# A fused attention and two-network kernel: readings of other engines' results in the first network listed half an item later

## The chip, the cores and the metric

One core of a Trainium2 chip runs the whole program. The metric is the device time of one execution in microseconds (us); the median of three runs is taken.

## The reference

Three layers run one after the other, all in float32. Shapes: batch 4, 8 heads, 768 positions, head dimension 48; so 3072 tokens of 384 numbers.

```
state = alpha[t][:, None] * state + outer(k[t], v[t]);  y[t] = q[t] @ state       # per batch and head
h = x @ w_in;  x1 = where(h > 0, h, exp(min(h, 0)) - 1) @ w_out                   # 384 -> 2048 -> 384
p = probs / (probs.sum(-1) + 1e-9)
out = sum over 4 experts e of p[:, e] * (relu(x1 @ w1[e]) @ w2[e])                # 384 -> 1024 -> 384
```

## The kernel before

**Precision.** A float32 matrix product is made of three products: each operand is kept as two parts, a rounded one ("hi") and what is left ("lo"), and hi x hi, hi x lo and lo x hi are added up in PSUM. `split` (L370) makes the parts: ScalarE (ACT) copies the source into hi (L372), VectorE (DVE) subtracts hi from the source into lo (L373).

**Tokens.** They are cut into 6 chunks of 512 (4 batches of 128 positions). A *unit* is one batch of one chunk in the attention layer. Chunk 0's four units run in a prologue. After it the first network runs as 96 *items*, 16 per chunk: item i is one block of 128 hidden numbers for the 512 tokens of a chunk. The attention units of chunk c run in between, in the items of chunk c - 1.

**An item** (loop at the end of `run`). `first` is 9 matmuls of 128x512 into one of three PSUM banks h0, h1, h2 (`g1`, L417). `elu` is two ACT activations (L426, L427) and one DVE operation (L428) that writes back into the bank. `parts` makes the hi part (ACT, L433) and the lo part (DVE, L434); the lo part is the bank's last reader. `second` is 9 matmuls (`g2a`, L443) on the parts of the item two before. The bank of an item is wanted again by the third `first` or key transpose after it.

**Order.** For TensorE (PE), DVE, ACT and GpSimd (POOL) the program order is the order of the list written here; only SyncE's (SP's) DMA queue is ordered by the scheduler. Work that reads another engine's result is put off with `later` (L119) and run by `flush` (L126). An item goes: `first`; flush; the steps of the slot (i, 0); `elu`; flush; `second`; the steps of the slot (i, 1); the `post` steps; `parts`. Every step goes through `do`, which flushes before it runs its functions; `post` steps go through `do` as well, so a `post` step is preceded by one more flush, and several in one item flush one another's put-off work at once.

**What the steps are.** (a) Attention, 6 steps per unit over the two slots of 13 items: `scores` and `ktrans` (PE; then masking on DVE and a copy on ACT), `prep0` (four scans on DVE, then three ACT activations in `inverse`), `prep1` (`newton`, three DVE operations), `xtrans` (the previous unit's result, split), `yout_t` and `state` (PE; then `pack`, an ACT copy L319, two writes to DRAM issued by ACT, and a read back by SP, and `decay`, two DVE operations), `prep2` (one DVE operation, q times P; the next step's `scores` read it). The fourth unit's `xtrans` stands in the slot (end - 1, 0), ahead of the next chunk's first item. (b) `conv_f64`, items 0 to 12: the first network's weights arrive as 64-bit numbers; ACT scales them (L403), DVE puts the bits together in three operations (L76, L79, L82), then a split. Beside each stands `load_f64`, the load of the block two further. (c) `prep_w`, items 20 to 92, a `post` step: 11 groups of the experts' weights are loaded, summed (DVE, L471; copies on ACT), split and stored: steps q0 to q4, then three w2 steps. The next group's load into the single buffer "wr" stands in the group's step 5. (d) `prep_x0` in the last 16 items, the first inputs of the second network, on POOL and ACT.

**After it.** The second network (`layer1`, `layer2`) runs with no put-off queue: `later` runs its function at once.

Of the kernel before, what the change touches and what calls it, by code (L numbers as in the profile page):

```python
# [8 lines left out]
F32 = mybir.dt.float32  # L9
# [3 lines left out]
ALU = mybir.AluOpType  # L13
AX = mybir.AxisListType

B, H, S, D = 4, 8, 768, 48
# [70 lines left out]
class _Fast:  # L87
# [206 lines left out]
    def yout_t(self, u):  # L294


        nc = self.nc
        c, b = u
        raw = self.raw[u]
        ps = self.abank()  # L300
        for a in range(NP):
            for j in range(2):
                r = slice(64 * j, 64 * j + D)
                nc.tensor.matmul(
                    ps[64 * j:64 * j + 64, a * C:(a + 1) * C], self.st[b][r, a, :], raw[r, Q0 + a * C:Q0 + (a + 1) * C],
                    start=(a == 0), stop=False, skip_group_check=True,
                )
        for a in range(NP):
            for j in range(2):
                h = 2 * a + j  # L310
                nc.tensor.matmul(
                    ps[64 * j:64 * j + D, a * C:(a + 1) * C], raw[:, V0 + h * D:V0 + (h + 1) * D],
                    self.sm[u, j][:, a, :], start=False, stop=True, skip_group_check=True,
                )
        del self.sm[u, 0], self.sm[u, 1]

        def pack():
            y = self.ap.tile([128, NP * C], F32, tag="y", name="yt")
            nc.scalar.copy(y[0:SW], ps[0:SW])  # L319
            for j in range(2):  # L320
                nc.scalar.dma_start(out=self.x0d[b][D * j:D * (j + 1)], in_=y[64 * j:64 * j + D])
            x = self.ap.tile([128, KD, C], F32, tag="y", name="xr")
            nc.sync.dma_start(
                out=x, in_=self.x0d[b].rearrange("(k r) (a t) -> (r a) k t", k=KD, a=NP)
            )
            self.y[u] = x

        self.later(pack)

    def state(self, u):  # L330
# [63 lines left out]
    def conv_f64(self, f):  # L394
        nc = self.nc
        t = self.wp.tile([128, 2 * DM], I32, tag="cv", name="cv", bufs=4)
        raw = self.raw64.pop(f)
        tf = t.bitcast(F32)
        if f % 2 == 0:
            j = f // 2  # L400
            self.w1[j] = self.big.tile([128, 2, 2, 2 * DM], F32R, tag=f"W{j}", name=f"w_W{j}")
        w = self.w1[f // 2]
        nc.scalar.mul(tf, raw[:, :, 1].bitcast(F32), REBASE)  # L403

        def bits():
            _f64_bits(nc, t, raw)
            self.split(w[:, 0, f % 2], w[:, 1, f % 2], tf)

        self.later(bits)

# [19 lines left out]
    def parts(self, h):  # L430
        nc = self.nc
        g = self.hp.tile([128, 2, 512], F32R, tag="g", name="g")
        nc.scalar.copy(g[:, 0], h)  # L433
        nc.vector.tensor_tensor(out=g[:, 1], in0=h, in1=g[:, 0].bitcast(F32), op=ALU.subtract)  # L434
        return g

    def g2a(self, w, fi, g, n, first, last):
# [11 lines left out]
    def prep_w(self, g, nxt):  # L449

        nc = self.nc
# [15 lines left out]
        def tile_w():  # L467
            return self.wp.tile([128, 3, 2, 128], F32R, tag="cv", name="wh", bufs=4)

        def tt(out, a, b, op):  # L470
            nc.vector.tensor_tensor(out=out, in0=a, in1=b, op=op)  # L471

        def end(c, q):
            t = tile_w()
            self.split(t[:, :, 0], t[:, :, 1], c)
            self.later(lambda: nc.sync.dma_start(out=self.wad[g][:, 3 * q:3 * q + 3], in_=t.bitcast(F32)))

        def w(k, n, m=1):
            v = st[0][:, n:n + m, k * 128:(k + 1) * 128]
            return v if m > 1 else v[:, 0]  # L480

        lo = lambda t, i, m=1: t[:, i:i + m] if m > 1 else t[:, i]
        tile_c = lambda: self.wp.tile([128, 3, 128], F32, tag="wc", name="wc", bufs=2)
        bc = lambda v, m: v.unsqueeze(1).to_broadcast([128, m, 128])
        add, sub = ALU.add, ALU.subtract

# [29 lines left out]
            end(t, 3)  # L516

        def q4():
            t = tile_w()
            a = st[0][:, 1, 128:384].rearrange("p (n d) -> p n d", n=2)  # L520
            self.split(t[:, 0:2, 0], t[:, 0:2, 1], a)
            c = tile_c()
            tt(c[:, 0], w(1, 1), st["u"], sub)
            self.split(t[:, 2, 0], t[:, 2, 1], c[:, 0])
            self.later(lambda: nc.sync.dma_start(
                out=self.wbd[g][:, 0:768], in_=t.bitcast(F32).rearrange("p n h d -> p (n h d)")
            ))

        def w2(n):
            t = self.wp.tile([128, 2, DM], F32R, tag="cv", name="wh2", bufs=4)  # L530
# [5 lines left out]
        s = [[(q, ())] for q in (q0, q1, q2, q3, q4)]  # L536
        s[0] += [(load, (1,))]
        s += [[(w2, (n,))] for n in range(3) if fs[n] is not None]
        if nxt:
            s[5] += [nxt]  # L540
        return (load, (0,)), s

    def load_x(self, r, m, out):
# [251 lines left out]
    def run(self):  # L795
        nc, tc = self.nc, self.tc
# [19 lines left out]
        seq = [self.unit_steps(units[i], units[i + 1] if i + 1 < len(units) else None) for i in range(len(units))]  # L816

        def do(step):
            if self.queue is not None:
                self.flush()  # L820
            for f, a in step:
                f(*a)

# [12 lines left out]
        for i in range(B + 1):  # L836
            u, w = units[i - 1], units[i]
# [24 lines left out]
        slots = {}  # L862
        for c in range(1, NCH):
            steps = [s for u in units[4 * c:4 * c + 4] for s in seq[units.index(u)]]
            end = F1 * c
            av = half(end - F1, end - 3)
            for n, s in enumerate(steps):
                k = av[n * len(av) // len(steps)]
                slots.setdefault(k, []).append(s)
                if n % 6 == 5:  # L870
                    slots[k].append([(load_next, ())])
            slots.setdefault((end - 1, 0), []).append([(self.xtrans, ((c, B - 1),))])

        def open_p2():
            self.attn.__exit__(None, None, None)
# [4 lines left out]
        at = lambda i, f, *a: post.setdefault(i, []).append((f, a))  # L880
        for f in range(nf, F1):
            at(f - nf, self.conv_f64, f)
            if f + 2 < F1:
                at(f - nf, self.load_f64, f + 2)
        b5 = n1 - F1
        at(b5 - 1, open_p2)
        at(F1 - 2, self.load_probs)
        at(F1 + 2, self.norm_probs)
        w0, w1 = WPREP
        load, wsteps = None, []  # L890
        for g in reversed(range(NG)):
            load, l = self.prep_w(g, load)
            wsteps = l + wsteps
        at(w0 - 2, do, [load])
        for n, s in enumerate(wsteps):
            at(w0 + n * (w1 - w0) // len(wsteps), do, s)
        for m in range(2):
            at(b5 + 7 + 8 * m, self.load_wa, m)
            at(b5 + 10 + 2 * m, self.load_wb, m)
# [10 lines left out]
        def first(it):  # L910
            c, f = it
            return self.g1(self.w1[f // 2], f % 2, self.x0[c], 0, 512)
# [18 lines left out]
        for i in range(n1):  # L931
            h = first(items[i])
            self.flush()
            for s in slots.pop((i, 0), []):
                do(s)
            self.elu(h)
            self.flush()
            if i >= LA:
                second(items[i - LA])
            for s in slots.pop((i, 1), []):  # L940
                do(s)
            for f, a in post.pop(i, []):
                do([(f, a)])
            gs[items[i]] = self.parts(h)
        self.flush()
        self.queue = None
        order.__exit__(None, None, None)
        assert not slots and not post and not loads
# [6 lines left out]
        for i in range(ng + 1):  # L955
            r, q = divmod(i, NG)
# [231 lines left out]
```

## Time and profile before

| | |
|---|---|
| median of 3 runs | 1349.61 us (1346.24 to 1351.78) |
| the profiled execution | 1350.88 us |
| its span | 1348.8 us |
| busy: PE, DVE, ACT, POOL | 94%, 66%, 43%, 39% of the span |
| mean granted TensorE clock | 0.975 |

The span is what the trace covers; 2.1 us of the execution lie around it. A busy share is a mean over the prologue (to 39 us), the first network (39 to about 605 us) and the second network (to the end). In the rows of a timeline a bracket gives the time that the engine was idle before the instruction and what ended it. DVE, ACT and PE run their lists in order, so one long wait holds back all that is listed behind it.

### The profile page before, as it was taken

To read this page: it belongs to the slowest core of one execution; us is meant where nothing else is said; L and a number is where in the kernel's file an instruction comes from. 1 tells how busy PE (TensorE), PEld (TensorE's weight loads), DVE (VectorE), ACT (ScalarE), POOL (GpSimd) and SP (SyncE) were. 2 spreads that over 40 slices of the span, in tenths; PEclk is the share of its full clock that TensorE was granted. 3 is DMA by queue.
4 is the path that set the end of the run, shared out by engine and by line. 5 is a ranking of instruction groups with operands and counts; after the bars stand their busy time and mean duration, and the time that the engine had idled before them with its cause. 6 is when DMAs were issued, how large, how long until landed. Compare 5 with 4: busy or idle time off the path is not lost.

```text
span 1348.8 us, 17699 instructions
## 1 busy us (share of the span) xinstructions
PE 1266.3 (94%) x6457; PEld 1021.3 (76%) x6457; DVE 891.6 (66%) x1510; ACT 585.0 (43%) x1076; POOL 520.0 (39%) x405
## 2 busy tenths in 40 slices
PE   8776899999899999999999999999999999999997
PEld 6554587777677778877888888778878878888886
DVE  8776667667666675656666675756676666666664
ACT  5454545645655655663433323243423332324231
POOL 0000000000000000558888565696865555547472
PEclk8888999989999999999999999999999999999999
DMA  6543235464465555573756546766463585434322
GB/s 222 184 140 120 97 114 182 143 215 150 173 215 175 193 172 168 214 267 110 261 208 226 183 157 238 291 242 247 161 260 117 201 319 179 160 137 161 136 97 81
DMA packets 71534, 246.70 MB, mean 183 GB/s; under 512 B 6680, under 2 KB 38264, under 8 KB 62096
## 3 DMA queue, kind: packets, MB, share of 16 engines
q1 hardware_dynamic: 68016, 236.84, 49.6%
q10 hardware_dynamic: 3424, 8.65, 1.7%
q8 instruction: 53, 0.87, 0.3%
q14 instruction: 41, 0.34, 0.1%
HBM read 182.11 MB, written 63.36 MB: 182 GB/s over the span
## 4 chain that ended last, share of the span: by engine, by line
PE 61%; DVE 16%; ACT 10%; issue 5%; POOL 4%; DMA 2%; ACTq 0%; SPq 0%; DVEq 0%; POOLq 0%
PE h L708 21%; PE t L758 12%; PE a L758 9%; PE h L417 6%; PE t L443 5%; PE h L758 4%; ACT g L433 2%; DVE P L202 2%; DVE h L428 2%; DVE u L728 2%; ACT wh L372 1%; ACT e L427 1%; DVE wh L373 1%; DVE sm L255 1%; DVE wc L471 1%
## 5 line engine op out<-in xcount | busy, mean ns | idle before, releaser
L417 PE MATMUL h<-x,w_W 128*128 128x512 f32 x864 | 229.9, 411 | 38.0 <-DVE g L434 29.8
L728 DVE TENSOR_TENSOR u<-h,u 128x512 f32<-128x512 f32 x258 | 177.6, 688 | 90.8 <-PE h L708 89.7
L417 PEld LDWEIGHTS h<-x,w_W 128*128 128x128 f32 x864 | 166.9, 197 | 82.3 <-DVE g L434 34.7
L708 PE MATMUL h<-xc_Q,wa 128*128 128x512 f32 x780 | 220.1, 392 | 5.0 <-DVE c L728 2.4
L443 PE MATMUL t<-g,w_W 128*128 128x512 f32 x864 | 217.9, 396 | 2.7 <-ACT g L433 1.5
L553 POOL TENSOR_TENSOR xs<-xr 128x512 f32<-128x512 f32 x8 | 10.4, 1300 | 538.5 <-ACT x1raw L917 538.5
L688 POOL TENSOR_TENSOR g_W<-c,g_W 128x512 fp32r<-128x512 f32 x128 | 164.4, 1300 | 125.9 <-ACT c L687 107.7
L686 ACT ACTIVATE g_W<-c 128x512 fp32r<-128x512 f32 x128 | 80.0, 626 | 276.8 <-DVE c L728 164.0
L443 PEld LDWEIGHTS t<-g,w_W 128*128 128x128 f32 x864 | 161.6, 189 | 41.1 <-ACT g L433 3.6
L708 PEld LDWEIGHTS h<-xc_Q,wa 128*128 128x128 f32 x780 | 146.1, 188 | 38.5 <-DVE u L728 4.3
L758 PE MATMUL t<-g_W,wb 128*128 128x512 f32 x576 | 157.6, 389 | 0.0
L434 DVE TENSOR_TENSOR g<-h,g 128x512 fp32r<-128x512 f32 x96 | 66.3, 690 | 92.5 <-ACT g L433 91.8
L758 PEld LDWEIGHTS t<-g_W,wb 128*128 128x128 f32 x576 | 108.0, 188 | 22.6 <-POOL g_W L688 0.2
L687 ACT ACTIVATE c<-c 128x512 f32<-128x512 f32 x192 | 121.0, 632 | 7.4
L728 DVE TENSOR_TENSOR c<-u,h 128x512 f32<-128x512 f32 x123 | 84.1, 686 | 51.0 <-PE h L708 37.9
L708 PE MATMUL h<-xc_W,wa 128*128 128x512 f32 x390 | 111.0, 393 | 5.4 <-DVE u L728 3.4
L758 PE MATMUL a<-g_W,wb 128*128 128x512 f32 x384 | 113.7, 395 | 0.6 <-POOL g_W L688 0.6
L722 DVE COPY u<-h 128x512 f32<-128x512 f32 x99 | 68.1, 691 | 68.4 <-PE h L708 68.1
L688 POOL TENSOR_TENSOR g_X<-c,g_X 128x512 fp32r<-128x512 f32 x64 | 82.2, 1296 | 62.6 <-ACT c L687 52.0
L686 ACT ACTIVATE g_X<-c 128x512 fp32r<-128x512 f32 x64 | 40.0, 627 | 142.6 <-DVE c L728 78.5
L428 DVE SCALAR_TENSOR_TENSOR h<-e,h 128x512 f32<-128x512 f32 x96 | 66.5, 693 | 44.5 <-ACT e L427 44.2
L708 PEld LDWEIGHTS h<-xc_W,wa 128*128 128x128 f32 x390 | 73.2, 189 | 23.2 <-DVE u L728 4.8
(138 smaller groups left out, 1939.4 us busy)
## 6 DMA issues: line engine op xcount, KB each, us to landing
wa<-wad SPq DMA_DIRECT2D x33, 1536.0 KB, 6.7
wb<-wbd SPq DMA_DIRECT2D x30, 1536.0 KB, 7.0
raw<-in_att_dram SPq DMA_DIRECT2D x22, 960.0 KB, 5.4
wad<-wh SPq DMA_DIRECT2D x44, 384.0 KB, 3.0
wbd<-wh SPq DMA_DIRECT2D x43, 384.0 KB, 3.7
xcd<-xh SPq DMA_DIRECT2D x30, 512.0 KB, 2.9
wraw<-in_wm_dram SPq DMA_DIRECT2D x16, 768.0 KB, 4.3
wraw<-in_we_dram SPq DMA_DIRECT2D x20, 576.0 KB, 4.4
```

The source lines that it names most:

```text
L202: nc.vector.tensor_tensor_scan(P[:, a, :], raw[:, A0 + a * C:A0 + (a + 1) * C], self.plo.to_broadcast([128, C]), 1.0, ALU.mult, ALU.max,)
L417: nc.tensor.matmul(h[:, 0:n], w[:, wl, fi, k * 128:(k + 1) * 128], x[:, xl, k, n0:n0 + n], start=(k == 0 and i == 0), stop=(k == KD - 1 an ...
L428: nc.vector.scalar_tensor_tensor(out=h, in0=e, scalar=-1.0, in1=h, op0=ALU.add, op1=ALU.max)
L434: nc.vector.tensor_tensor(out=g[:, 1], in0=h, in1=g[:, 0].bitcast(F32), op=ALU.subtract)
L443: nc.tensor.matmul(self.xa[k][:, 0:n], w[:, wl, fi, DM + k * 128:DM + (k + 1) * 128], g[:, gl, 0:n], start=(first and i == 0), stop=(last ...
L686: nc.scalar.activation(out=g[:, n, 0], in_=v, func=AF.Relu)
L687: nc.scalar.activation(out=v, in_=v, func=AF.Relu)
L688: nc.gpsimd.tensor_tensor(out=g[:, n, 1], in0=v, in1=g[:, n, 0].bitcast(F32), op=ALU.subtract)
L708: nc.tensor.matmul(b, w[:, wl], x[:, xl], start=(j == 0), stop=(j == 2))
L722: nc.vector.tensor_copy(out, b)
L728: (nc.vector if "b" in (a0, a1) or dst == "S5" else nc.gpsimd).tensor_tensor(out=out, in0=val(a0, b), in1=val(a1, b), op=ALU.add if op == ...
L758: nc.tensor.matmul(oa[m, d], wt[:, f, wl, d * 128:(d + 1) * 128], G[m][:, f, gl], start=first, stop=last)
```

## The change

The loop of items and the attention slots stay. What is changed: `do` and `post` no longer flush, so put-off work runs only at the two flushes of an item, and work that is put off inside put-off work waits for the next flush again. The lo part of an item's result is put at the head of the queue. The split of a converted weight block, and the splits of the experts' weight sums, are put off once more (sum, then hi, then lo, then the store, at four places). The sums' steps move from `post` into the slots. The fourth unit's `xtrans` moves to (end - 2, 1). The next group's weight load moves from step 5 to step 6. The small buffers "wc" go from two to four. The two writes of `pack` are issued by SP instead of ACT. One flush is added ahead of the closing of the attention buffers, and the last flush is repeated until the queue is empty.

```diff
@@ pack, in yout_t
-                nc.scalar.dma_start(out=self.x0d[b][D * j:D * (j + 1)], in_=y[64 * j:64 * j + D])
+                nc.sync.dma_start(out=self.x0d[b][D * j:D * (j + 1)], in_=y[64 * j:64 * j + D])
@@ conv_f64
         def bits():
             _f64_bits(nc, t, raw)
-            self.split(w[:, 0, f % 2], w[:, 1, f % 2], tf)
+            self.later(lambda: self.split(w[:, 0, f % 2], w[:, 1, f % 2], tf))
@@ parts
         nc.scalar.copy(g[:, 0], h)
-        nc.vector.tensor_tensor(out=g[:, 1], in0=h, in1=g[:, 0].bitcast(F32), op=ALU.subtract)
+        self.queue.insert(
+            0, lambda: nc.vector.tensor_tensor(out=g[:, 1], in0=h, in1=g[:, 0].bitcast(F32), op=ALU.subtract)
+        )
@@ prep_w
         def end(c, q):
-            t = tile_w()
-            self.split(t[:, :, 0], t[:, :, 1], c)
-            self.later(lambda: nc.sync.dma_start(out=self.wad[g][:, 3 * q:3 * q + 3], in_=t.bitcast(F32)))
+            def parts():
+                t = tile_w()
+                self.split(t[:, :, 0], t[:, :, 1], c)
+                self.later(lambda: nc.sync.dma_start(out=self.wad[g][:, 3 * q:3 * q + 3], in_=t.bitcast(F32)))
+
+            self.later(parts)
...
-        tile_c = lambda: self.wp.tile([128, 3, 128], F32, tag="wc", name="wc", bufs=2)
+        tile_c = lambda: self.wp.tile([128, 3, 128], F32, tag="wc", name="wc", bufs=4)
...
         def q4():
-            t = tile_w()
             a = st[0][:, 1, 128:384].rearrange("p (n d) -> p n d", n=2)
-            self.split(t[:, 0:2, 0], t[:, 0:2, 1], a)
             c = tile_c()
             tt(c[:, 0], w(1, 1), st["u"], sub)
-            self.split(t[:, 2, 0], t[:, 2, 1], c[:, 0])
-            self.later(lambda: nc.sync.dma_start(
-                out=self.wbd[g][:, 0:768], in_=t.bitcast(F32).rearrange("p n h d -> p (n h d)")
-            ))
+
+            def parts():
+                t = tile_w()
+                self.split(t[:, 0:2, 0], t[:, 0:2, 1], a)
+                self.split(t[:, 2, 0], t[:, 2, 1], c[:, 0])
+                self.later(lambda: nc.sync.dma_start(
+                    out=self.wbd[g][:, 0:768], in_=t.bitcast(F32).rearrange("p n h d -> p (n h d)")
+                ))
+
+            self.later(parts)
...
         if nxt:
-            s[5] += [nxt]
+            s[6] += [nxt]
@@ run
         def do(step):
-            if self.queue is not None:
-                self.flush()
             for f, a in step:
                 f(*a)
...
-            slots.setdefault((end - 1, 0), []).append([(self.xtrans, ((c, B - 1),))])
+            slots.setdefault((end - 2, 1), []).append([(self.xtrans, ((c, B - 1),))])
...
+        at(b5 - 1, self.flush)
         at(b5 - 1, open_p2)
...
         for n, s in enumerate(wsteps):
-            at(w0 + n * (w1 - w0) // len(wsteps), do, s)
+            k = 2 * w0 + n * 2 * (w1 - w0) // len(wsteps)
+            slots.setdefault((k // 2, k % 2), []).append(s)
...
             for f, a in post.pop(i, []):
-                do([(f, a)])
+                f(*a)
             gs[items[i]] = self.parts(h)
-        self.flush()
+        while self.queue:
+            self.flush()
```

## Rows read from the trace of the kernel before

**Rows 1.** The page, busy time of an engine: us, share, instructions.
```profile
PE 1266.3 (94%) x6457; PEld 1021.3 (76%) x6457; DVE 891.6 (66%) x1510; ACT 585.0 (43%) x1076; POOL 520.0 (39%) x405
```

**Rows 2.** Busy time by stretch: length, PE, PEld, DVE, ACT, POOL, granted clock, DMA.
```profile
39.13:163.43 124.30, 87.17 (x527) 65.15 (x526) 89.29 (x137) 59.89 (x102) 0.00 (x0) 0.89 0.41 139
...
168.86:605.40 436.54, 414.74 (x2484) 334.01 (x2483) 288.89 (x588) 250.19 (x512) 35.62 (x27) 0.98 0.54 184
```

**Rows 3.** Waits of PE, 39 to 165 us: us in total, times, longest.
```profile
PE h L417 <- DVE g L434: 21.6, 6, 9.3
```

**Rows 4.** Waits of DVE, 39 to 165 us.
```profile
DVE g L434 <- ACT g L433: 18.1, 13, 2.3
DVE cv L76 <- ACT cv L403: 9.0, 4, 3.0
```

**Rows 5.** Timeline, all engines, 72 to 82 us: start, duration, instruction.
```profile
72.69 1.36 DVE L202 TENSOR_TENSOR_SCAN P<-raw,plo 128x128 f32<-128x128 f32 x4
74.08 0.63 ACT L210 ACTIVATE lnP<-P 128x512 f32<-128x512 f32 x1 [3.06 <-DVE P L202]
...
76.13 0.87 ACT L403 ACTIVATE cv<-wraw 128x768 f32<-128x768 f32 x1
77.03 0.56 DVE L76 TENSOR_SCALAR cv<-cv 128x768 int32<-128x768 int32 x1 [2.98 <-ACT cv L403]
...
79.61 0.83 ACT L372 CAST w_W<-cv 128x768 fp32r<-128x768 f32 x1 [2.61 <-DVE cv L82]
80.35 0.58 ACT L433 CAST g<-h 128x512 fp32r<-128x512 f32 x1
...
80.96 0.69 DVE L434 TENSOR_TENSOR g<-h,g 128x512 fp32r<-128x512 f32 x1 [1.38 <-ACT g L433]
...
81.71 4.21 PE L417 MATMUL h<-x,w_W 128*128 128x512 f32 x9 [7.17 <-DVE g L434]
```

**Rows 6.** Groups of instructions by line: count, busy us, mean ns.
```profile
L350 DVE TENSOR_TENSOR st<-tmp,P 128x192 f32<-128x192 f32 x16 | 5.7, 359 | 0.6
```

**Rows 7.** Waits of PE, 168.86 to 615 us.
```profile
PE h L417 <- DVE g L434: 8.2, 6, 3.4
PE a L247 <- ACT e L427: 7.5, 3, 2.6
PE h L417 <- DVE x L373: 3.5, 4, 1.6
PE a L247 <- issue: 2.2, 1, 2.2
```

**Rows 8.** Timeline, 287 to 289 us and 226 to 228 us.
```profile
287.91 0.69 DVE L434 TENSOR_TENSOR g<-h,g 128x512 fp32r<-128x512 f32 x1 [2.71 <-ACT g L433]
...
288.66 4.21 PE L417 MATMUL h<-x,w_W 128*128 128x512 f32 x9 [3.36 <-DVE g L434]
...
226.25 0.69 DVE L237 TENSOR_TENSOR raw<-raw,P 128x512 f32<-128x512 f32 x1
...
227.04 1.16 PE L247 MATMUL a<-raw 48*128 48x128 f32 x16 [2.64 <-ACT e L427]
```

**Rows 9.** The chain that ended last: start, us, what.
```profile
518.55 2.04 PE h L417 x9
```

**Rows 10.** DMA issues: KB each, median us to landing.
```profile
raw<-in_att_dram SPq DMA_DIRECT2D x22, 960.0 KB, 5.4
...
wraw<-in_we_dram SPq DMA_DIRECT2D x20, 576.0 KB, 4.4
...
xr<-x0d SPq DMA_DIRECT2D x20, 192.0 KB, 2.5
```

**Rows 11.** The writes of `pack` (L321), by source line: issue to landing.
```profile
DMA to landing us min/median/max: 1.9/4.7/6.3
```

**Rows 12.** SP's own waits, 39 to 605 us; and a pair of ACT's issues in the timeline.
```profile
SPq L323 <- DMA x0d<-yt: 104.5, 20, 6.9
...
63.66 0.82 ACTq L321 DMA_DIRECT2D x0d<-yt  x2
```

## The prediction

> **What bounds the kernel now.** I read the page's busy times first: PE is busy for 94% of the span [rows 1], so a gain can come only from PE's idle time, from stretches at the lower clock, or from a stretch in which another engine leads. The diff touches the first network alone, so I then cut that network with the table of stretches [rows 2]. The reader is to see two different halves. In the first, 124.3 us up to the last converted weight block, PE is busy for 87.2 us and DVE for 89.3: neither is full, and DVE has the larger load. In the second, 436.5 us up to the end of the network, PE is busy for 414.7 us and idle for 21.8, at a mean granted clock of 0.98.
>
> The lists of waits say who holds what. In the first half PE loses most to h banks that the lo subtraction has not yet given back, 21.6 us in 6 waits of up to 9.3 [rows 3]. DVE's own idle time there is 34.6 us by its list of waits (124.3 - 89.3 gives 35.0), of which 18.1 stand ahead of that same lo subtraction, waiting for ACT's hi copy, and 9.0 ahead of the bit operations, waiting for ACT's scaling [rows 4]. The timeline shows why [rows 5]: DVE runs the scans; ACT, which has the three activations of the inverse listed next, sits idle for 3.06 us until they are done, then does them, then the scaling, while DVE is idle for 2.98; then DVE does the bits while ACT is idle for 2.61 in front of the hi copy of the weights; only behind that stands the item's hi copy, and PE has by then waited 7.17 us for the bank. DVE and ACT take turns instead of working side by side.
>
> **The change, part by part.** *Conversion, and hi of an item.* Before, scaling, bits and weight hi all stand ahead of the item's hi copy, in one go. After, ACT lists only the scaling ahead of it; the bits run in the next item's first flush, the weight hi in its second, the weight lo one flush later. Nothing is added to DVE: the same 89.3 us of work [rows 2]. What idle time stays? From the end of an item's bits ACT must do the weight hi (0.83), the next scaling (0.87) and the item's hi copy (0.58), 2.28 us with the rows' durations [rows 5], before DVE's lo subtraction can start. Meanwhile DVE has the item's L428 operation (about 0.69, as long as its lo subtraction) and the slot's attention work: the scans (1.36) [rows 5] and a masking, or newton's three operations of about 0.69, or, in the poorest item, the decay (two of 0.36) [rows 6] and q times P, again one of about 0.69: 1.4 + 0.69 = 2.1 us. So two item types in three are covered, up to the small attention copies on ACT (some 0.3 us over), and the third leaves about 1 us: 1.5 us per unit, 6 for four units. I add 3 us for the items at either end of the half, which have no attention work as cover, and 1 for DVE behind PE's scores. That leaves 10 of the 35 us: **25 us gained**. Upper bound: all 34.6. Lower bound: only the 9.0 in front of the bits and a third of the 18.1 go, 15 us. PE does not become the bound there: 87.2 us of work against 99.
>
> *The second half.* PE leads, so only its idle time and the lower clock can be recovered. Its waits by name are 8.2 us for h banks, 7.5 and 2.2 us ahead of scores, 3.5 us for the lo part of a new chunk's input [rows 7], 21.4 of the 21.8. The first kind is seen at 287 to 289 us [rows 8]: ACT has waited for the scans and done the inverse with the item's hi copy listed behind it, as in [rows 5], so that DVE idles 2.71 us and PE 3.36. After the change the inverse runs in the next item's first flush, behind the hi copy. The second kind is put down to ACT, but the row above it shows q times P ending at 226.94 and the scores starting at 227.04: it is DVE that was late, behind lo subtractions that waited for ACT. The third kind goes with the earlier xtrans. Behind the long waits PE runs slowly: nine matmuls take 4.21 us after the wait of 3.36 [rows 8], against 2.04 in the undisturbed run of groups [rows 9], which is what half of the full clock gives. The mean clock of 0.98 over 414.7 us of work prices that at 8.3 us (6 to 10 with the rounding). Without the waits most of it goes too. I leave 4 us of idle time and 2 us of clock: 21.8 + 8.3 - 6 = **24 us gained**. Bounds: 10 (half of the idle time stays and the clock with it) to 30. Idle time of DVE that lies under a busy PE gives nothing, so I count none.
>
> *What could be late next.* The chain per item from one L428 to the next runs through the hi copy, the put-off ACT work, L426 and L427. It is longest in the item behind the scans: masking and scans (2.7), inverse (three of 0.63 and their handing over, 1.9 to 2.3), the two activations (of that size, 1.2), L428 (0.7), some 7 us, and 3 to 5 us in the two others, so about 15 us in three items. PE needs (436.5 - 21.8 - 8.3) / 80 = 5.1 us for an item, 15.2 for three [rows 2]; that just fits, and PE's lead of an item takes up the unevenness. This is why 4 us stay.
>
> *The load at step 6.* It now has two steps instead of three before the next group's first sum. 87 steps lie over 72 items, so two steps are 1.65 items, 6.7 us at two groups of 2.04 per item [rows 9] and 8.4 at 5.1. The load takes 4.4 us [rows 10], hidden unless SP is held: SP waits up to 6.9 us in front of the read-back [rows 12], once in three or four items. DVE's sum would then be up to 4.6 us late; PE's lead covers some 3 of that. I take 2 us for all groups, with ends 0 and 15.
>
> *The writes from SP.* Forty issues leave ACT, 0.82 us a pair [rows 12], 16 us of ACT time that stood ahead of casts; it is hidden now that ACT works beside DVE, so 0. SP gets the same issues; it waits for the read-back in any case. The four "wc" buffers and the extra flush cost no instruction. The store of a weight tile is listed up to half an item later (2.5 us), which four "cv" buffers cover at 0.83 item per step. Nothing of the second network changes.
>
> **Sum.** 25 + 24 - 2 = 47 us. Against the profiled execution (span 1348.8 and 2.1 around it, 1350.9) that gives 1304; the median of the runs is 1.3 lower, so I forecast **1303**.
>
> **The rivals.** *One: the writes land behind the unit load (slower).* Place: SP's queue, at every `pack`. ACT's cast in xtrans stands two items behind, 10.2 us at 5.1. The path to it is copy 0.59, issues 0.82, landing 4.7 [rows 11], issue 0.4, landing 2.5 [rows 10]: 9.0 us. On SP's queue the writes may be issued right behind the next unit's 960 KB load, 5.4 us to landing [rows 10]; if they begin only after it, the path is 14.4 us, and ACT, and with it PE, stands 4.2 us in each of 20 units: 84 us. 1304 + 84 = 1388. It decides once the writes take over 5.9 us to land. Against it: they contend with that load already and never took over 6.3 [rows 11], and PE's lead covers a part. By the Trainium skill (DMA: Bandwidth & Descriptors, Queues, rings and completion order) a DMA engine takes turns between queues but works one queue's descriptors off in ring order, which is this mechanism; no row here shows two dependent transfers on one queue. Chance 0.06.
>
> *Two: DVE's idle time only moves.* If the chain through ACT paces the items in the first half, each of the 16 keeps 1 us or more and 15 us are gained there; in the second half idle time is halved and the long waits still pull the clock, 10 us. 1351 - 25 + 2 = 1328. For it: the chain above fits only just. Against: two thirds of DVE's idle time have one cause, which is removed. Chance 0.2.
>
> *Three: everything goes.* 34.6 + 30 = 65 us, 1286. Chance 0.12.
>
> *Four: the change does not do what it says.* DVE's place for the lo subtraction hardly moves: it was last in its item and is first in the next. If ACT's order mattered as little, nothing would be gained, 1350. But ACT's order does change, by what stood ahead of the hi copy [rows 5, 8]. Chance 0.03.
>
> **How the numbers follow.** The forecast (1290 to 1318) has 0.59. The range leaves out rival one, rival four and the far ends of two and three: **1286 to 1331**. About 0.5%, 7 us, is what a measurement of this kernel can tell from no change. Faster by more: 0.59 + 0.2 + 0.12, and a little off for the far end of rival two, 0.90. Slower: 0.06. Within: 0.04.
>
> **What would show it.** Right: the first ACT copy of chunk 0's end some 25 us earlier; DVE's wait in front of L434 falling from 18.1 in the first half to a few us; no PE wait of over 3 us for an h bank; a mean clock of 0.99 in the second half; the second network as long as before. Wrong: DVE waits of the old size in front of L428 (rival two), ACT waits in front of the xtrans cast for a DMA (rival one), DVE waits in front of L471 for the weight load, or a second network that has grown.

## The result and the profile after

The median fell from 1349.08 us (1346.24 to 1351.78; 4 runs, one more than in the table above) to 1297.16 us (1294.27 to 1300.14, 4 runs): a ratio of 0.9616, interval 0.9586 to 0.9645. The profiled execution of the changed kernel took 1300.14 us.

The page of the changed kernel, busy times, granted clock, and the chain that ended last:

```profile
PE 1249.2 (96%) x6457; PEld 1013.5 (78%) x6457; DVE 896.5 (69%) x1510; ACT 585.6 (45%) x1076; POOL 521.5 (40%) x405
...
PEclk8998999999999999999999999999999999999999
...
PE 78%; DVE 9%; ACT 4%; POOL 3%; issue 3%; DMA 1%; SPq 0%; POOLq 0%; ACTq 0%; DVEq 0%
```

The instructions are the same as in [rows 1], and PE's busy time is 17 us less: matmuls that ran at the lower clock run at the full one. To see where the time went, the trace is cut at three marks that every kernel has: the start of the first `first` (L417), the last lo part of a converted weight (DVE, tile w_W), and the last `first`. The first two rows give the marks of the changed kernel (39.2, 142.6, 544.0):

```profile
L417 PE MATMUL h<-x,w_W x864: 387/389/796, 39.2 to 544.0; 128*128 128x512 f32 x173
...
L373 DVE TENSOR_TENSOR w_W<-cv,w_W x16: 945/948/953, 30.1 to 142.6; 128x768 fp32r<-128x768 f32 x16
```

| kernel | first half | second half | both | to the end | median, us | ratio to before, interval |
|---|---|---|---|---|---|---|
| before | 123.4 | 432.8 | 556.2 | 753.5 | 1349.08 | |
| **after** | 103.4 | 401.4 | 504.8 | 754.3 | 1297.16 | 0.9616 (0.9586 to 0.9645) |
| e1 | 116.3 | 420.7 | 537.0 | 752.2 | 1330.58 | 0.9874 (0.9828 to 0.9921) |
| e2 | 112.0 | 405.2 | 517.2 | 751.7 | 1309.65 | 0.9712 (0.9666 to 0.9758) |
| e3 | 116.1 | 402.7 | 518.8 | 750.7 | 1310.15 | 0.9717 (0.9669 to 0.9765) |
| e4 | 103.3 | 432.7 | 536.0 | 755.5 | 1331.60 | 0.9869 (0.9821 to 0.9918) |
| e5 | 105.6 | 402.8 | 508.4 | 755.5 | 1304.71 | 0.9666 (0.9626 to 0.9706) |
| e6 | 103.4 | 404.8 | 508.2 | 756.0 | 1302.66 | 0.9656 (0.9621 to 0.9691) |
| e7 | 97.3 | 400.8 | 498.1 | 755.5 | 1292.03 | 0.9581 (0.9544 to 0.9617) |
| e8 | 96.5 | 404.7 | 501.2 | 750.6 | 1293.41 | 0.9599 (0.9559 to 0.9639) |
| e9 | 104.5 | 402.4 | 506.9 | 749.7 | 1296.57 | 0.9612 (0.9573 to 0.9652) |
| e10 | 103.2 | 397.4 | 500.6 | 750.3 | 1291.99 | 0.9583 (0.9542 to 0.9624) |
| e11b | 94.4 | 404.7 | 499.1 | 750.9 | 1289.84 | 0.9566 (0.9528 to 0.9604) |
| e11 | 94.9 | 396.5 | 491.4 | 750.0 | 1281.59 | 0.9504 (0.9467 to 0.9542) |

The change gained 20.0 us in the first half and 31.4 in the second, 51.4 together; the rest stayed (+0.8). The ratio of each experiment is to runs of the kernel before that were taken beside it (medians 1347.25 to 1348.18). The rest moves by up to 6 us between kernels none of which edits it, so an effect of a few microseconds is read from the halves and not from the median. The halves are of one profiled execution each; where an edit leaves a half alone (e4, e6, e10 the first, e3 and e7 the second), that half came out at 103.2 to 103.4 and at 400.8 to 402.7 us, which gives an idea of what they can tell. The table of stretches, cut as in [rows 2]: length, PE, PEld, DVE, ACT, POOL, granted clock, DMA.

```profile
39.25:143.59 104.34, 83.55 (x527) 64.51 (x526) 88.60 (x138) 60.17 (x104) 0.00 (x0) 0.93 0.50 164
148.80:553.70 404.90, 400.87 (x2476) 326.67 (x2475) 294.92 (x588) 251.39 (x511) 37.10 (x27) 1.00 0.58 198
```

DVE's idle time in the first half is 104.34 - 88.60 = 15.7 us where it was 35.0 by the same subtraction; PE's in the second is 4.0 where it was 21.8, and the clock there is 1.00. The waits of the changed kernel: first DVE's and PE's between 39 and 145 us, then PE's, ACT's and DVE's between 145 and 562.

```profile
DVE g L435 <- ACT g L433: 14.4, 11, 2.9
...
PE a L247 <- issue: 8.5, 2, 8.0
PE h L417 <- DVE w_W L373: 7.0, 4, 2.9
PE h L417 <- DVE g L435: 4.1, 3, 2.2
...
PE t L445 <- DVE g L435: 3.5, 2, 2.5
...
ACT wh L372 <- DVE wc L473: 29.3, 21, 2.8
...
DVE wc L473 <- DMA wraw<-in_we_dram: 6.2, 2, 4.3
```

The wait in front of the bits [rows 4] is gone, and PE's 21.6 us for an h bank [rows 3] are 4.1. What is left of DVE's waits stands in front of the same lo subtraction (now L435), and PE has no wait of over 3 us for a bank any more. The timeline of all engines at 92 to 100.5 us shows one of the largest:

```profile
91.95 1.36 DVE L202 TENSOR_TENSOR_SCAN P<-raw,plo 128x128 f32<-128x128 f32 x4
92.06 0.83 ACT L372 CAST w_W<-cv 128x768 fp32r<-128x768 f32 x1 [3.62 <-DVE cv L82]
...
93.23 0.67 DVE L428 SCALAR_TENSOR_TENSOR h<-e,h 128x512 f32<-128x512 f32 x1
93.34 0.63 ACT L210 ACTIVATE lnP<-P 128x512 f32<-128x512 f32 x1 [0.45 <-DVE P L202]
...
95.39 0.87 ACT L403 ACTIVATE cv<-wraw 128x768 f32<-128x768 f32 x1
96.17 0.57 ACT L433 CAST g<-h 128x512 fp32r<-128x512 f32 x1
...
96.77 0.69 DVE L435 TENSOR_TENSOR g<-h,g 128x512 fp32r<-128x512 f32 x1 [2.87 <-ACT g L433]
...
98.38 1.86 PE L417 MATMUL h<-x,w_W 128*128 128x512 f32 x7 [2.89 <-DVE w_W L373]
```

The three activations of the inverse still stand ahead of the hi copy here. The 24 steps of a chunk's four units are laid over 26 half-item slots, so the steps shift by one slot after the second unit: the scans of the first two units stand in an item's second slot, those of the last two in its first. From there the second flush of the same item runs the inverse, ahead of `parts`. Both waits of 2.87 us in this half, at 96.77 and 121.67 us, are of these two units. Each is followed by two more waits, of 1.1 and 0.96 us, so all three items of such a unit wait; in each of the first two units only one item in three does, for 0.80 us.

### The profile page after: what moved, and what is told of

Read it like the earlier page. It is cut to its first block, busy times and chain, and to the rows that moved or that the text cites. A ratio compares the mean times of both kernels' runs of the same rounds, so it can differ in the third digit from the quotient of the medians.

```text
span 1298.3 us, 17667 instructions
## 1 busy us (share of the span) xinstructions
PE 1249.2 (96%) x6457; PEld 1013.5 (78%) x6457; DVE 896.5 (69%) x1510; ACT 585.6 (45%) x1076; POOL 521.5 (40%) x405
## 4 chain that ended last, share of the span: by engine, by line
PE 78%; DVE 9%; ACT 4%; POOL 3%; issue 3%; DMA 1%; SPq 0%; POOLq 0%; ACTq 0%; DVEq 0%
PE h L717 22%; PE t L767 13%; PE h L417 12%; PE t L445 12%; PE a L767 9%; PE h L767 4%; DVE u L737 1%; PE a L247 1%; PE a L304 1%; PE a L311 1%; DVE w_W L373 1%; DVE cv L79 1%; DVE cv L82 1%; DMA xraw<-x1d 1%; POOL g_W L697 1%
## 5 line engine op out<-in xcount | busy, mean ns | idle before, releaser
L417 PE MATMUL h<-x,w_W 128*128 128x512 f32 x864 | 219.8, 398 | 11.6 <-DVE w_W L373 7.0
L445 PE MATMUL t<-g,w_W 128*128 128x512 f32 x864 | 214.8, 392 | 3.5 <-DVE g L435 3.5
L417 PEld LDWEIGHTS h<-x,w_W 128*128 128x128 f32 x864 | 161.4, 190 | 50.4 <-DVE w_W L373 10.4
L737 DVE TENSOR_TENSOR c<-u,h 128x512 f32<-128x512 f32 x123 | 84.1, 686 | 51.7 <-PE h L717 37.9
L428 DVE SCALAR_TENSOR_TENSOR h<-e,h 128x512 f32<-128x512 f32 x96 | 66.5, 693 | 74.0 <-ACT e L427 74.0
L435 DVE TENSOR_TENSOR g<-h,g 128x512 fp32r<-128x512 f32 x96 | 65.9, 686 | 41.1 <-ACT g L433 40.7
```

Of the source, the lines that this page charges most:

```text
L417: nc.tensor.matmul(h[:, 0:n], w[:, wl, fi, k * 128:(k + 1) * 128], x[:, xl, k, n0:n0 + n], start=(k == 0 and i == 0), stop=(k == KD - 1 an ...
L428: nc.vector.scalar_tensor_tensor(out=h, in0=e, scalar=-1.0, in1=h, op0=ALU.add, op1=ALU.max)
L435: 0, lambda: nc.vector.tensor_tensor(out=g[:, 1], in0=h, in1=g[:, 0].bitcast(F32), op=ALU.subtract)
L445: nc.tensor.matmul(self.xa[k][:, 0:n], w[:, wl, fi, DM + k * 128:DM + (k + 1) * 128], g[:, gl, 0:n], start=(first and i == 0), stop=(last ...
L737: (nc.vector if "b" in (a0, a1) or dst == "S5" else nc.gpsimd).tensor_tensor(out=out, in0=val(a0, b), in1=val(a1, b), op=ALU.add if op == ...
```

## The experiments

The first six undo one part of the change or do one alone; the last six ask what the waits that are left are worth. Four parts were not undone by themselves: the lo part at the head of the queue, the sums' steps in the slots, the load at step 6 and the four "wc" buffers.

**e1: the kernel before with the new listing alone** (no flush in front of a step; conversions, sums, lo subtraction, writes and slots as before).

```diff
         def do(step):
-            if self.queue is not None:
-                self.flush()
             for f, a in step:
...
             for f, a in post.pop(i, []):
-                do([(f, a)])
+                f(*a)
```

> The kernel before, with one thing changed: steps no longer flush, so put-off work runs at the item's two flushes only. No added stage, writes on ACT, sums still among the post steps. Theory (the gain needs the added stage too): the bits and the weight block's hi copy now stand in one flush, so ACT waits for 2.5 us of bits with the next item's two activations listed behind it; DVE then idles some 2 us in each of 13 items, and the first half gains only 5 to 12 us of the 20 it gained; the second half gains 10 to 20 of its 31. Time 1318 to 1335. Rival (the flushes are all of it, the stages add nothing): 1297 to 1303.

Measured 1330.58 us, as expected: 7.1 us gained in the first half and 12.1 in the second. The listing is not the whole change; the rest of it carries more than half of the gain. Its waits, DVE's at 38 to 156 us and ACT's at 145 to 600:

```profile
DVE h L428 <- ACT e L427: 24.2, 14, 2.5
...
ACT wh L372 <- DVE wc L471: 75.5, 34, 4.9
```

DVE's wait has moved from the lo subtraction to L428, which is the sign that rival two gave.

**e2: the changed kernel with the flush in front of every step put back.**

```diff
         def do(step):
+            if self.queue is not None:
+                self.flush()
             for f, a in step:
...
             for f, a in post.pop(i, []):
-                f(*a)
+                do([(f, a)])
```

> The changed kernel, but every step flushes again before it runs. All stages are kept. Theory: a flush inside an item runs the put-off work ahead of the item's hi copy again, so the first half loses 10 to 18 us and the second 5 to 15; time 1312 to 1330. Rival (the stages are all of it, where they are flushed does not matter): 1297 to 1302.

1309.65 us, on the expected side and smaller: 8.6 us back in the first half and 3.8 in the second. DVE's waits at 38 to 156 us name the bits again, once per unit, as in [rows 4]:

```profile
DVE cv L76 <- ACT cv L403: 8.0, 4, 3.0
```

**e3: the conversion's split at once,** behind its bits.

```diff
-            self.later(lambda: self.split(w[:, 0, f % 2], w[:, 1, f % 2], tf))
+            self.split(w[:, 0, f % 2], w[:, 1, f % 2], tf)
```

> The changed kernel, but the weight block's hi copy stands right behind the bits again (one stage less). Theory: ACT waits for the bits ahead of the next item's activations, DVE waits for those: 1 to 2 us in each of 13 items, all in the first half, 12 to 25 us; time 1309 to 1322, waits of DVE in front of L428 in the first half from 0.7 to over 10 us. Rival (DVE has other work meanwhile): 1297 to 1301.

1310.15 us, as expected: 12.7 us back in the first half, which at 116.1 is that of e1 (116.3). So the first half's 20.0 us are about 7 for the listing and 13 for the put-off weight hi. DVE's and PE's waits at 38 to 156 us:

```profile
DVE h L428 <- ACT e L427: 24.1, 14, 2.5
...
PE a L247 <- issue: 22.3, 3, 11.1
```

**e4: the sums' splits at once,** in the step that computes them.

```diff
         def end(c, q):
             def parts():
...
-            self.later(parts)
+            parts()
...
         def q4():
...
-            self.later(parts)
+            parts()
```

> The changed kernel, but the hi copies of the experts' weight sums stand right behind the sums again, in the slot. Theory: ACT waits for the sums ahead of the item's own operations, its waits on L473 rise from 29 us to over 50; PE's lead of one item covers most of it, so 2 to 10 us are lost, all in the second half: 1299 to 1307. Rival (no lead left, each wait reaches PE): over 1312. Second rival (wholly covered): 1297.

1331.60 us: my theory fell and the rival held. The second half took 432.7 us, that of the kernel before (432.8): without this one stage the other edits are worth nothing there. ACT's waits at 145 to 580 us, then all engines at 332 to 340:

```profile
ACT wh L372 <- DVE wc L473: 77.2, 32, 4.7
...
333.74 1.36 DVE L202 TENSOR_TENSOR_SCAN P<-raw,plo 128x128 f32<-128x128 f32 x4
...
335.53 0.28 DVE L473 TENSOR_TENSOR wc<-wraw 128x128 f32<-128x128 f32 x1
...
335.89 0.51 ACT L372 CAST wh<-wc 128x384 fp32r<-128x384 f32 x1 [3.79 <-issue]
336.31 0.58 ACT L433 CAST g<-h 128x512 fp32r<-128x512 f32 x1
...
336.92 0.69 DVE L435 TENSOR_TENSOR g<-h,g 128x512 fp32r<-128x512 f32 x1 [1.11 <-ACT g L433]
...
337.66 2.93 PE L417 MATMUL h<-x,w_W 128*128 128x512 f32 x6 [2.98 <-DVE g L435]
```

ACT stands 3.79 us because the copy of the sum is listed, the sum is listed on DVE behind the scans, and the item's hi copy is listed behind the copy. (The trace names no releaser for it; the sum ends at 335.81, 0.08 us before the copy starts.) PE pays 2.98 us for it and then runs matmuls at the lower clock (2.93 us for six). The kernel before has this wait too (ACT's waits there, 165 to 600 us), a row that the prediction had not read:

```profile
ACT wh L372 <- DVE wc L471: 54.3, 30, 4.9
```

The wait alone does not make the loss. In e1, where the sums stand among the `post` steps, ACT waits for them as long (75.5 us), and the second half is 12.0 us shorter than here, where the sums stand in the slots. Which part of the 31.3 us belongs to the stage and which to the sums' place is not shown: no run put the sums off and left them in `post`.

**e5: the writes of `pack` issued by ACT again.**

```diff
-                nc.sync.dma_start(out=self.x0d[b][D * j:D * (j + 1)], in_=y[64 * j:64 * j + D])
+                nc.scalar.dma_start(out=self.x0d[b][D * j:D * (j + 1)], in_=y[64 * j:64 * j + D])
```

> The changed kernel, with the two writes of each unit's result issued by ACT again. Theory: 16 us of issue time go back to ACT, hidden beside DVE and under PE's lead: 0 to 3 us, 1296 to 1300. Rival (ACT's issue time stood on the path): 8 to 16 us, 1305 to 1313. Second rival (on SP's queue the writes land behind the 960 KB loads, so going back helps): 1285 to 1294, and waits of ACT for the read-back in the changed kernel's trace.

1304.71 us, above what the theory gave and just under the first rival; the halves grew by 2.2 and 1.4 us. The intervals of e5 and of the changed kernel overlap, so the move is worth between nothing and a few microseconds. That going back helps (the second rival) fell with it. SP's waits in the changed kernel, 39 to 562 us, show the read-back held for less than half of the time in [rows 12], in 20 waits again; since SP now issues the writes itself and comes to the read-back later, this alone does not say that the writes land sooner:

```profile
SPq L323 <- DMA x0d<-yt: 45.1, 20, 5.6
```

**e6: the fourth unit's `xtrans` back in the slot (end - 1, 0).**

```diff
-            slots.setdefault((end - 2, 1), []).append([(self.xtrans, ((c, B - 1),))])
+            slots.setdefault((end - 1, 0), []).append([(self.xtrans, ((c, B - 1),))])
```

> The changed kernel, with the fourth unit's xtrans in its old slot, one step nearer to the next chunk's first item. Theory (its lo part is then the last thing that the chunk waits for, as before: 3.5 us in four waits): 3 to 7 us with the lower clock behind them, all in the second half; 1300 to 1304. Rival (the half item that the put-off subtraction is late makes it worse): over 1306. Second rival (DVE no longer late there): 1297.

1302.66 us, as expected, though its interval overlaps that of the changed kernel: 3.4 us in the second half, where PE again waits at the start of each of the five chunks, as in [rows 7]. The waits themselves hold 1.9 us of it (PE's waits, 145 to 562 us):

```profile
PE h L417 <- DVE x L373: 1.9, 5, 0.8
```

**e7: the scaling of a weight behind the item's hi copy.**

```diff
+            late = []
             for f, a in post.pop(i, []):
-                f(*a)
+                if f in (self.conv_f64, self.load_f64):
+                    late.append((f, a))
+                else:
+                    f(*a)
             gs[items[i]] = self.parts(h)
+            for f, a in late:
+                f(*a)
```

> The changed kernel, with the scaling of a weight block (0.89 us on ACT) listed behind the item's hi copy instead of ahead of it, and the load beside it likewise. Theory (what is left of DVE's idle time in the first half, 14.4 us in front of L435, is the 0.83 + 0.89 + 0.57 us that ACT needs from the end of the bits): each of 11 waits falls by up to 0.9 us; the first half ends 5 to 9 us earlier, 1288 to 1293. Rival (DVE then waits for the scaling in front of the bits instead, or PE is what holds): 1296 to 1300.

1292.03 us, as expected, the first half 6.1 us shorter. DVE's waits in front of L435 fell from 14.4 us; up to the end of this kernel's half (37 to 135 us) they are:

```profile
DVE g L435 <- ACT g L433: 7.8, 8, 2.2
```

**e8: the inverse behind the hi copy also where the scans stand in an item's first slot:** there it is put off once more.

```diff
-        self.later(inverse)
+        self.later((lambda: self.later(inverse)) if self.first_half else inverse)
...
-        self.later(newton)
+        self.later((lambda: self.later(newton)) if self.inv_late else newton)
```

> The changed kernel; where prep0 stands in the first slot of an item, its three ACT activations are put off once more, behind the item's hi copy, and newton likewise. Theory (the two waits of 2.87 us in front of L435 are these activations): both fall under 1 us, 3 to 5 us in the first half, little in the second where PE leads; 1292 to 1295. Rival (the activations then hold up the next item's L426 and DVE waits in front of L428 by as much): 1296 to 1299.

1293.41 us, as expected, but by other sums: the first half is 6.9 us shorter instead of 3 to 5, and the second 3.3 longer, where PE now waits 1.2 and 0.9 us ahead of scores, behind ACT. Both waits of 2.87 us fell to 0.65, and the 1.1 us behind each went too. DVE's waits for the hi copy up to the end of this half (39 to 137 us), and those in front of the old L428, where the rival wanted them and where nothing came up (the lines stand one lower in this kernel):

```profile
DVE g L436 <- ACT g L434: 7.2, 8, 1.6
DVE h L429 <- ACT e L428: 0.6, 2, 0.3
```

**e9: the scores' preparation two steps earlier.** In the changed kernel PE stands 8.0 us in one piece ahead of the first half's last scores. What is moved is `prep2`, q times P, one operation of DVE; the text below calls it scores and exponentials, which is not what the step holds.

```diff
-        s.append([(self.xtrans, ((u[0], u[1] - 1),))] if u[1] else [])
+        s.append(N(self.prep2) + ([(self.xtrans, ((u[0], u[1] - 1),))] if u[1] else []))
...
-        s.append(N(self.prep2))
+        s.append([])
```

> The changed kernel with one step moved: the scores and exponentials of a unit's heads that stand at the end of its list (prep2) come two steps earlier, in the step of the transposed copies. In the changed kernel's first half TensorE stands 8.0 us in one piece in front of the last unit's scores (at 110.26 us), because nothing of the weights is ready there. My theory: that stand is DVE's work list showing on TensorE, not the scores' own lateness, so that the 8.0 us move to other places and the time gains little: 1293 to 1298 us (0 to 4 us under the changed kernel), first half 99 to 104 us against 103.4. The rival, that the late step itself costs them: the stand goes, first half under 98 us, 1286 to 1291 us. A second rival: the earlier scores make ScalarE's exponentials stand in front of the conversions, first half over 105 us, 1299 to 1304 us.

1296.57 us, by my theory: PE's long stand is gone and the first half is no shorter (104.5 us, just above the range). PE's two largest waits at 38 to 143 us, once 8.5 and 7.0, are now:

```profile
PE h L417 <- DVE w_W L373: 7.4, 5, 2.1
PE h L417 <- DVE g L435: 4.9, 4, 2.3
```

A further 4.0 us in 3 waits stand ahead of scores behind ACT's copy of `pack`. PE's idle time moves from place to place while DVE's list takes as long.

**e10: the sums ended before GpSimd's work begins.**

```diff
-WPREP = (20, 92)
+WPREP = (20, 80)
```

> The changed kernel with the weights' sums spread over items 20 to 80 instead of 20 to 92, so that they end before GpSimd's work begins (at about 480 us). In the changed kernel the subtractions of DVE whose operands lie all in SBUF take 1.26 to 1.68 us beside GpSimd's work and 0.28 to 0.55 us before it, and DVE is late for TensorE there (0.95 + 2.54 us in front of the multiplications of the second layer). My theory: the stretched operations come from the overlap, so these two waits go and the second half is shorter by 2 to 4 us (397.5 to 399.5 us against 401.4): 1293 to 1296 us. The rival, that the denser sums cost DVE the slack it has between 150 and 480 us: new waits of TensorE on DVE there, second half over 403 us, 1298 to 1306 us.

1291.99 us, a little under the forecast; the second half is 4.0 us shorter and PE waits for no lo subtraction there any more, as the theory had it. (The interval overlaps that of the changed kernel; the stretch decides.) The median fell by more than the half did, since the rest took 750.3 us as well; why the rest varies stays open.

**e11b: e7 and e8 together; e11: e7 to e10 together.** The diffs are those above.

> The changed kernel with both earlier edits that put ScalarE's work behind the hi copy: the scaling of a converted weight behind it, and the inverse of the units that stand in the item's first slot put off once more. Alone they gave 6.1 us of the first half and about 4 to 6 us. My theory: they shorten different waits of DVE on the hi copy (the 0.9 us of the scaling in most items, the 2.87 us of two items), and add up to most of their sum: 1286 to 1290 us, waits of DVE on the hi copy under 6 us of the first half's 14.4. The rival, that DVE's own work is the bound once one of them is done: 1290 to 1293 us, no better than either alone.

1289.84 us, at the top of what the theory gave, the first half 9.0 us shorter where the parts alone gave 6.1 and 6.9. They add up in part: DVE's waits up to the end of this half (38 to 133 us) fell to

```profile
DVE g L436 <- ACT g L434: 4.2, 6, 0.8
DVE h L429 <- ACT e L428: 1.4, 4, 0.4
```

DVE is busy for 88.5 us of 95.4 (37.9 to 133.25 us), so 6.8 us of idle time are all that a new order could still take from this half. The median cannot be told from those of e7 and e8 (the intervals overlap).

> All four edits on the changed kernel: scaling behind the hi copy, inverse put off once more, the scores two steps earlier, the sums ended before GpSimd's work. My theory: the first two add up (1286 to 1290 us), the third gives 0 to 4 us and the fourth 2 to 4 us more: 1280 to 1287 us. The rival, that the third and the fourth fill the slack that the first two made: over 1288 us.

1281.59 us, ratio 0.9504 (0.9467 to 0.9542), clear of the changed kernel's interval: it beats both kernels. Its table of stretches, columns as above:

```profile
37.10:132.00 94.90, 84.09 (x527) 64.49 (x526) 87.41 (x137) 59.64 (x103) 0.00 (x0) 0.95 0.54 177
132.00:528.50 396.50, 395.51 (x2455) 323.22 (x2456) 278.89 (x585) 251.86 (x512) 34.27 (x27) 1.00 0.58 199
```

PE is idle for 1.0 us of the second half, so nothing is left there for a new order. Against e11b the second half is 8.2 us shorter, twice what e10 gave alone; the waits ahead of scores that e8 had brought are gone too. Whether the earlier preparation of the scores removes them was not run by itself.

## Why the prediction was right, and where a step was off

The forecast was 1303 us in a range of 1286 to 1331, the measurement 1297.16. The sum was 25 + 24 - 2 = 47 us; by the trace it was 20.0 + 31.4 + 0, less 0.8 in the rest. One half is 5 us under its term and the other 7 over: that the total lies nearer than its parts is luck.

**First half, 25 predicted, 20.0 measured.** The turn-taking of DVE and ACT [rows 5] went, and DVE's work stayed (88.60 us against 89.29), as said. The step that failed is the idle time left to DVE: I took 10 us, from two covered item types in three; it was 15.7, nearly all of it in front of L435 (14.4 us up to 145 us). So the sign that I had given, that wait falling from 18.1 to a few us, did not come: it fell by 3.7. Most of the gain is the 9.0 us in front of the bits and the waits beside the two of [rows 4], 7.5 us (34.6 - 18.1 - 9.0), of which 1.3 are left. The cover was worked out for an inverse that always runs in the next item's first flush. For half of the units it runs in the same item's second flush, ahead of the hi copy, at 2.87 us a time, and the two items behind then wait as well: 4.9 us per unit where I had 1.5. In the other two units the cover held: one item in three waits 0.8 us, between the 0.5 that the terms give (2.28 + 0.3 - 2.1) and the 1 that I took. e8 takes the late inverse away and gains 6.9 us. That the scaling ahead of the hi copy also costs was in the prediction, within the 1.5 us per unit, 6 in all; e7, which takes away the scaling alone, gains 6.1.

**Second half, 24 predicted, 31.4 measured, above the bound of 30.** The idle time came out as said: 21.8 us became 4.0, and I had left 4. The mis-sized term is the clock. I priced the lower clock at 8.3 us and left 2 of it, a gain of 6.3; PE's busy time fell by 414.74 - 400.87 = 13.9 us. Eight matmuls fewer lie in that stretch, 1.3 us at 0.16 each, so some 12.5 us are left to explain. The mean of 0.98 was rounded: cut into stretches of 1 us, the kernel before loses 10.2 us there to the lower clock (9.5 if only PE's busy time is counted) and the changed kernel nothing. The last two to three microseconds are in part the number of waits, 16 before and 3 after. A matmul takes 0.39 us, but in a run of nine (2.20 us) one ends every 0.23, so each break in the run adds some 0.16 us of busy time, about 2 us for 13; this is an estimate.

Where the gain comes from was argued wrongly. I credited it to the inverse, to q times P and to the earlier `xtrans`. The last is borne out (3.4 us in e6, of it 1.9 in PE's waits; 3.5 predicted). But the stage added to the sums was no term of the sum at all, and e4 shows that without it, with the sums in the slots, the half gains nothing. Nor are the parts additive: the listing alone gives 12.1 us (e1), all without the sums' stage 0.1 (e4), all of it 31.4. The 4.0 us that stay are also not the chain behind the scans, as I had it: 3.5 of them are two waits of PE beside GpSimd's work, which e10 removes.

**The load at step 6, 2 us predicted, 0 measured.** DVE did wait for it, 6.2 us in 2 waits of up to 4.3, close to the 4.6 worked out; PE's lead covered it whole. **The writes from SP** were set at 0; e5 puts them between nothing and a few microseconds of gain.

**The rivals.** One fell: in the changed kernel's second half ACT has one wait for a read-back (1.2 us) and one put down to the writes (2.3 us), and PE none. By the source line the writes took a median of 4.0 us to land where it had been 4.7 [rows 11]; the longest took 8.5, beyond the 5.9 at which the rival was to decide, but the waits stayed at these two. The Trainium skill (DMA: Bandwidth & Descriptors, Queues, rings and completion order) has one queue's descriptors worked off in ring order; no run here shows whether the slowest writes stood behind a load. Two fell for the change, though it is what e1 and e3 look like: there DVE's idle time did move to L428. Three (everything goes, 1286) is passed by e11 alone, with edits that the change does not have. Four fell: the listing alone (e1) gains.

## What to carry to other kernels

Where two engines each run a list written in advance, look for operations that wait for the other engine and stand ahead of the operation that frees a buffer: what is to be put off is each such reading, and one reading left in place (the sums here, where they stand among the steps ahead of an item's own work) can hold back all that the others give. Work out for every phase of a repeated pattern in which flush its put-off work lands, since a shift by half an item puts it back ahead of what it should follow. A long wait of the engine that only follows is no gain by itself: remove it alone, as in e9, and it comes up elsewhere.

## What the runs showed of the hardware

I had not expected DVE's sums to become slow late in the first network. The groups of DVE instructions of the changed kernel, by line and form, at 478 to 545 us (count, busy us, mean ns, then idle time before):

```profile
L435 DVE TENSOR_TENSOR g<-h,g 128x512 fp32r<-128x512 f32 x16 | 11.0, 688 | 7.3 <-ACT g L433 7.3
...
L373 DVE TENSOR_TENSOR wh<-wc,wh 128x384 fp32r<-128x384 f32 x8 | 7.4, 928 | 0.0
L373 DVE TENSOR_TENSOR wh<-wraw,wh 128x384 fp32r<-128x384 f32 x5 | 6.4, 1278 | 0.0
...
L473 DVE TENSOR_TENSOR ut<-wraw 128x128 f32<-128x128 f32 x2 | 1.7, 832 | 0.0
```

The same in e10, where the sums end before, at 420 to 482 us:

```profile
L373 DVE TENSOR_TENSOR wh<-wraw,wh 128x384 fp32r<-128x384 f32 x8 | 4.4, 552 | 0.0
L373 DVE TENSOR_TENSOR wh<-wc,wh 128x384 fp32r<-128x384 f32 x8 | 4.4, 550 | 0.0
```

GpSimd idles until 484 us in the changed kernel and then runs operations of about 1.3 us. Beside them a subtraction of DVE with both operands in SBUF takes 0.93 or 1.28 us on the mean instead of 0.55. The lo subtraction, which is larger and has one operand in PSUM, keeps its 0.69. That it is GpSimd, and not the time of the run, shows operation by operation in the timeline (490 to 491 and 513 to 516 us): a subtraction with no GpSimd operation beside it keeps its 0.55 us, and one that starts within such an operation ends 0.41 us behind its end (515.33 and 514.92), as if it had stood for nearly all of it.

```profile
490.86 0.55 DVE L373 TENSOR_TENSOR wh<-wc,wh 128x384 fp32r<-128x384 f32 x1
...
513.62 1.30 POOL L373 TENSOR_TENSOR xc_Q<-xs,xc_Q 128x512 fp32r<-128x512 f32 x1
...
513.92 1.41 DVE L373 TENSOR_TENSOR wh<-wc,wh 128x384 fp32r<-128x384 f32 x1
```

The timeline of PE in the changed kernel shows the price:

```profile
525.17 2.11 PE L445 MATMUL t<-g,w_W 128*128 128x512 f32 x8 [0.95 <-DVE g L435]
...
532.08 2.11 PE L445 MATMUL t<-g,w_W 128*128 128x512 f32 x8 [2.54 <-DVE g L435]
```

In e10 both waits are gone. The Trainium skill (SBUF — State Buffer, Who interferes with whom) says that a DVE instruction with two SBUF inputs contends with a GpSimd instruction that reads SBUF, and that one with at most one SBUF input does not, outside the modes that use two ports; the rows agree with both (0.55 to 1.28 us, and 0.69 unchanged).
